# Transposing the softmax weights on TensorE instead of by DMA in the odd head pairs of the first batch

## The chip, the cores and the metric

The kernel runs on one core of a Trainium2 chip. The metric is the device time of one execution in microseconds. It is given as the median of runs; a profile comes from one further execution.

## What is computed

The reference is attention with RMS-normalised queries and keys, followed by a two-layer network with ELU. There are 8 batches, 12 heads, 448 positions and a head size of 64; the network goes from 768 to 2048 and back to 768.

```python
q_n, k_n = rmsnorm(q, g_q), rmsnorm(k, g_k)
scores = matmul(q_n, k_n.T) / sqrt(64)
attn = exp(scores - max(scores))
attn = attn / (sum(attn) + 1e-9)
x = matmul(attn, v)                # then heads side by side: 3584 x 768
h = x @ w_in
g = where(h > 0, h, exp(min(h, 0)) - 1)
out = g @ w_out
```

## The kernel before, in words

All products are made from float16 numbers in two parts, a high one and a low one that holds what the high one lost. Three products (high by high, high by low, low by high) stand for one in float32.

**Attention.** Heads are taken in pairs, 6 pairs to a batch, 48 in all. A pair has 896 query rows, cut into 7 chunks of 128. A chunk T passes through these steps, each on its engine: `s_mm` (TensorE, the scores into a PSUM bank), `s_max` (VectorE, L547), `s_exp` (ScalarE, L553, in place, with the row sum), `s_z` (GpSimd, L557, the sum scaled), `s_rec` (VectorE, L564, 1/z), `s_hi` (ScalarE, L571, the high part of the weights times 1/z), `s_lo` (VectorE, L576, the low part) and `s_tr` (SP, L586, a DMA transpose of both parts into `pts`, the keys on partitions). A pair's transposes go into two buffers, one a head, which the next pair takes over once `attend` has read them. `attend(p)` (TensorE, L597) multiplies the transposed weights by v into the bank `av`, in 22 products of 64 output rows; `x_high` (ScalarE, L604) and `x_low` (VectorE, L608) then read `av`.

**Weights.** The network's weights are converted in the kernel, `w_in` in 16 tiles (`conv_in`) and `w_out` in 24 (`conv_out`). Each is loaded, decoded (`s_act`, ScalarE, L230 and L231), put together (`s_join` and `s_sign`, VectorE, L236 and L260), and summed by column on TensorE (`s_sums`, L135) into columns 448 to 511 of a bank; `s_scale` takes the largest sum (VectorE, L138) and makes a scale from it. From the eighth tile of `w_out` on this bank is `av`, whose columns 0 to 447 belong to `attend`.

**The network.** Its products for one batch (`mlp`, L682 and L696) are spread over the attention of the next batch, from half step 92 on. ScalarE and VectorE make g from each bank (L621 to L637).

**Order.** The program is a list of half steps h, two to a chunk and 14 to a pair. In every half step each engine's work is written in a fixed order: loads; the steps of the chunks (the maximum in even half steps, the exponential in odd ones, `s_hi` two chunks behind in the even ones, `s_lo` in the odd ones); other tasks by a table of half steps (`at`, `steps_at`); then on TensorE the network's products, `s_mm` and `attend`; then TensorE's own tasks (`s_sums` and others). Engines take their lists in order, and SP, which issues all DMAs, does too. `attend(p)` is in half step 7 of the next pair, `x_high` in 8, `x_low` in 9. `s_sums` of every fourth tile of `w_out` is in half step 6 and its `s_scale` in 8. Score banks: 5 in the first batch, 4 afterwards. In the first batch the untransposed weights lie in 8 buffers in `gall`, later in a ring of 3 (`p16`).

The stretches of the profile below are called by pairs: pair 0 begins with the first maximum at 23 us, pair 1 at 46, pair 3 at 90, pair 5 at 133, pair 6 (the second batch) at 157, pair 7 at 185, pair 8 at 216, pair 9 at 245 and pair 10 at 273. A chunk's later steps fall into the stretch after its maximum, and so does `attend`.

Of the kernel before, what the change touches and what calls it, by code (L numbers as in the profile page):

```python
# [32 lines left out]
def tile_attention_then_elu_mlp(ctx: ExitStack, tc: tile.TileContext, qk, v, v_scan, gg, w_in, w_out, out):  # L33
# [12 lines left out]

    nc = tc.nc
# [16 lines left out]
    def t_s(T):  # L64
        return sb[T % (5 if T < PB else 4)]
# [42 lines left out]
    pfirst = cols(gall, NF)[8:]  # L108
# [102 lines left out]
    def conv(src, i, width, acol, bank, parts):  # L211
# [47 lines left out]
        def s_sign():  # L259
# [6 lines left out]
            (-(10, 6, 7)[min(max(i - 2, 0), 2)] if width == WI_W else 0 if i == 1 else -1, load), (3, s_act), (4, s_join), (5, s_sign), (6, on_pe(s_sums)),  # L266
            (7 if width == WI_W else 8, s_scale),
# [6 lines left out]
    def conv_in(f):  # L274
        hi, lo = (t[f].rearrange("p c n -> p (c n)") for t in (whi, wli))
        half = [slice(0, 384), slice(384, 768)]
        dgw = None
        pss = [None, None]

        def s_diag(w, ws):  # L280
            nonlocal dgw
# [16 lines left out]

        return conv(

            w_in, f, WI_W, a_in[:, f : f + 1], sb[4 - f] if f < 2 else av,
            [(9, s_diag), (9, s_high), (11, on_pe(s_low)), (12, lambda w, ws: s_out(0)),
             (13, lambda w, ws: s_out(1))],
        )

    def conv_out(i):
# [22 lines left out]
        def s_store(w, ws):  # L329
# [4 lines left out]
            [(9, s_mult), (10, s_high), (11, s_low), (12, s_store)],  # L334
# [6 lines left out]
    vscale, mscale, vpow = {}, {}, {}  # L341

# [151 lines left out]
    def m_scale(b):  # L494

        p2 = vpow[b]
        if b == 0:
            ibits(a_in, a_in, POWER, ALU.bitwise_and, 0, ALU.bitwise_or)  # L500
        am = small("am")
        nc.vector.tensor_reduce(out=am, in_=a_in, axis=AX.X, op=ALU.max)
        sc, isc = small("sc", NF), small("isc", NF)
        gsc = small("gsc", NF)
        nc.vector.tensor_scalar(
            out=sc, in0=a_in, scalar1=p2, scalar2=2.0 ** (-28 - UP), op0=ALU.mult, op1=ALU.mult
        )
        ibits(isc, sc, -1, ALU.mult, 254 * E, ALU.add)
        nisc = small("nisc", NF)
        nc.vector.tensor_scalar(out=nisc, in0=isc, scalar1=-1.0, scalar2=None, op0=ALU.mult)  # L510

        u = small("u", bufs=3)
        nc.vector.tensor_scalar(
            out=u, in0=am, scalar1=p2, scalar2=2.0 ** (-12 - UP), op0=ALU.mult, op1=ALU.mult
        )
        ui = small("ui")
        ibits(ui, u, -1, ALU.mult, 254 * E, ALU.add)
        nc.vector.tensor_scalar(out=gsc, in0=sc, scalar1=ui, scalar2=None, op0=ALU.mult)
        mscale[b] = [sc, isc, nisc, gsc, u]
# [30 lines left out]

    def s_exp(T):
        ps, st = pss[T][:, :S], stats[T]
        nc.scalar.activation(ps, ps, AF.Exp, bias=st[:, 0:1], accum_out=st[:, 1:2])  # L553

    def s_z(T):
        st = stats[T]
        nc.gpsimd.tensor_scalar(  # L557
            out=st[:, 1:2], in0=st[:, 1:2], scalar1=1e-9, scalar2=2.0**-7, op0=ALU.add, op1=ALU.mult
# [186 lines left out]
    for b in range(B):  # L745
# [5 lines left out]
        at(HB * (b + 1), m_scale, b)  # L751
# [24 lines left out]
    for h in range(H0, LAST):  # L776
# [3 lines left out]
        if odd:  # L780
# [31 lines left out]
        for k in range(parts):  # L812
# [58 lines left out]
```

## Time and profile before

| | us |
|---|---|
| median of 3 runs | 1283.19 (1283.15 to 1283.57) |
| the profiled execution | 1282.81 |
| span of its profile | 1280.8 |
| TensorE busy | 1190.4 (93%) |
| ScalarE busy | 877.9 (69%) |
| VectorE busy | 857.5 (67%) |
| GpSimd busy | 534.7 (42%) |

The span runs from the first to the last instruction of the profiled execution. Busy time is the time in which an engine has an instruction in work; for TensorE the ends of products are modelled. In the rows PE is TensorE (PEld its loading of weights), DVE is VectorE, ACT is ScalarE, POOL is GpSimd, and SP issues DMAs; L and a number is a line of the kernel; `out<-in` names what an instruction writes and reads. PEclk is the clock granted to TensorE as a share of 2.4 GHz. A wait names the instruction that ended it.

### The profile page before, as it was taken

Reading aid. Unit: us, or ns where it says so; the run is one execution under the profiler, and the core shown is the slowest. Engines: PE = TensorE matmul, PEld = TensorE weight load, DVE = VectorE, ACT = ScalarE, POOL = GpSimd, SP = SyncE. Lnnn points to the kernel's source line nnn. Section 1 sums busy time; section 2 is a strip of 40 time slices with the busy share of each in tenths; the row PEclk is TensorE's granted clock in tenths of the full one; section 3 lists DMA queues with packets and bytes.
Section 4 is the critical chain, followed back from the end, with each engine's and each line's share of the span. In section 5 each row is a group of like instructions: output and inputs, shape, how many; then the busy total and the mean of one; then the engine's idle time right before and its main releaser. Section 6 shows DMA issues by size and latency. Waiting matters only on the chain.

```text
span 1280.8 us, 21526 instructions
## 1 busy us (share of the span) xinstructions
PE 1190.4 (93%) x6976; PEld 718.8 (56%) x6976; DVE 857.5 (67%) x1913; ACT 877.9 (69%) x1889; POOL 534.7 (42%) x843
## 2 busy tenths in 40 slices
PE   3667478899999999999999999999999999999998
PEld 2334144466555765577556755576557755676576
DVE  7878988986777567756686567756775768642310
ACT  6898869984788558865796578855886579643520
POOL 3676866674444343343434443434334344320000
PEclk9878679999999999999999999999999999999999
DMA  8999988889877997889788986799678977663011
GB/s 276 223 234 245 231 185 191 201 210 244 161 142 149 229 190 138 153 188 211 151 157 164 221 166 146 146 211 203 135 161 172 213 160 159 140 148 80 1 48 62
DMA packets 452559, 219.22 MB, mean 171 GB/s; under 512 B 408672, under 2 KB 428768, under 8 KB 452448
## 3 DMA queue, kind: packets, MB, share of 16 engines
q1 hardware_dynamic: 452448, 217.86, 78.1%
q8 instruction: 55, 0.90, 0.3%
q14 instruction: 56, 0.46, 0.1%
HBM read 93.52 MB, written 14.16 MB: 84 GB/s over the span
## 4 chain that ended last, share of the span: by engine, by line
PE 76%; DVE 14%; ACT 5%; DMA 3%; issue 2%; SPq 0%; POOL 0%; ACTq 0%; DVEq 0%
PE m L696 21%; PE m L682 20%; PE s L682 10%; PE s L696 9%; PE s L540 8%; PE av L597 7%; DVE w32s L260 2%; DMA pt<-p 2%; DVE wts L236 2%; DVE st L547 2%; DVE p L576 1%; ACT w32s L231 1%; DVE gall L576 1%; ACT wts L230 1%; DVE gall L637 1%
## 5 line engine op out<-in xcount | busy, mean ns | idle before, releaser
L547 DVE TENSOR_REDUCE st<-s 128x1 f32<-128x448 f32 x336 | 208.4, 620 | 174.0 <-PE s L540 173.0
L557 POOL TENSOR_SCALAR st<-st 128x1 f32<-128x1 f32 x336 | 87.4, 260 | 554.8 <-ACT s L553 551.4
L682 PE MATMUL m<-x,whi 128*128 128x448 f16 x1020 | 280.9, 352 | 1.4 <-DVE e L629 1.4
L696 PE MATMUL m<-gall,whos 128*128 128x448 f16 x1024 | 281.7, 353 | 0.0
L571 ACT ACTIVATE p<-s,st 128x448 f16<-128x448 f32 x294 | 186.0, 633 | 112.9 <-DMA pt<-p 89.5
L696 PEld LDWEIGHTS <-whos 128*128 128x128 f16 x1536 | 221.6, 145 | 72.4
L553 ACT ACTIVATE s<-s,st 128x448 f32<-128x448 f32 x336 | 203.2, 605 | 64.5 <-DVE st L547 58.9
L682 PEld LDWEIGHTS <-whi 128*128 128x128 f16 x1536 | 150.2, 98 | 140.7 <-issue 4.5
L576 DVE SCALAR_TENSOR_TENSOR p<-s,st,p 128x448 f16<-128x448 f32 x294 | 196.5, 668 | 31.2 <-ACT p L571 30.0
L540 PE MATMUL s<-qkt 128*128 128x448 f16 (+1 forms) x768 | 188.1, 366 | 16.4 <-DVE gall L576 10.3
L696 PE MATMUL m<-gall,wls 128*128 128x448 f16 x512 | 181.3, 354 | 0.0
L682 PE MATMUL m<-x,wli 128*128 128x448 f16 x510 | 179.9, 353 | 0.0
L682 PE MATMUL s<-x,whi 128*128 128x448 f16 x516 | 141.8, 352 | 0.9 <-DVE e L629 0.9
L696 PE MATMUL s<-gall,whos 128*128 128x448 f16 x512 | 141.2, 353 | 0.4 <-DVE gall L637 0.4
L696 PEld LDWEIGHTS <-wls 128*128 128x128 f16 x768 | 110.5, 144 | 42.7 <-issue 8.2
L597 PE MATMUL av<-pt,vt 128*64 128x448 f16 x1056 | 114.6, 364 | 3.9 <-DVE a_in L138 2.0
L682 PEld LDWEIGHTS <-wli 128*128 128x128 f16 x768 | 75.1, 98 | 74.6 <-issue 7.5
L637 DVE SCALAR_TENSOR_TENSOR gall<-e,gsc,gall 128x448 f16<-128x448 f32 x128 | 97.3, 760 | 29.1 <-ACT gall L634 29.0
L540 PEld LDWEIGHTS <-qkt 128*128 128x128 f16 (+1 forms) x768 | 63.4, 102 | 84.8 <-issue 39.4
L634 ACT ACTIVATE gall<-e,gsc 128x448 f16<-128x448 f32 x128 | 85.1, 665 | 17.8 <-DVE e L629 17.7
L604 ACT ACTIVATE x<-av 128x448 f16<-128x448 f32 x48 | 26.1, 545 | 103.6 <-PE av L597 103.6
L625 ACT ACTIVATE e<-e,nisc,isc 128x448 f32<-128x448 f32 x128 | 96.9, 757 | 0.3
(110 smaller groups left out, 1715.3 us busy)
## 6 DMA issues: line engine op xcount, KB each, us to landing
wls<-wl_d SPq DMA_DIRECT2D x48, 512.0 KB, 4.0
nat<-in_qk SPq DMA_DIRECT2D x48, 448.0 KB, 3.7
raws<-in_w_out SPq DMA_DIRECT2D x24, 512.0 KB, 4.3
qkt<-qkt SPq DMA_DIRECT2D x96, 112.0 KB, 2.3
out<-y SPq DMA_DIRECT2D x48, 224.0 KB, 2.5
vn<-in_v SPq DMA_DIRECT2D x38, 256.0 KB, 3.6
vscan<-in_v_scan SPq DMA_DIRECT2D x36, 224.0 KB, 3.8
whos<-in_w_in SPq DMA_DIRECT2D x10, 768.0 KB, 5.1
```

Of the source, the lines that this page charges most:

```text
L540: nc.tensor.matmul(ps[r0 : r0 + n, :S], lhs, qq[:, 1, h * S : h * S + S], start=(t == 0), stop=(t == 2),)
L547: nc.vector.tensor_reduce(out=st[:, 0:1], in_=pss[T][:, :S], axis=AX.X, op=ALU.max, negate=True)
L553: nc.scalar.activation(ps, ps, AF.Exp, bias=st[:, 0:1], accum_out=st[:, 1:2])
L557: nc.gpsimd.tensor_scalar(out=st[:, 1:2], in0=st[:, 1:2], scalar1=1e-9, scalar2=2.0**-7, op0=ALU.add, op1=ALU.mult)
L571: nc.scalar.activation(p16[:, :S], pss[T][:, :S], AF.Copy, scale=stats[T][:, 2:3])
L576: nc.vector.scalar_tensor_tensor(out=p16[:, S:], in0=ps[:, :S], scalar=r, in1=p16[:, :S], op0=ALU.mult, op1=ALU.subtract)
L597: nc.tensor.matmul(av[64 * h : 64 * h + 64, :S], vt[p][:, j + NJ * i, h], pt[h][:, j, :], start=(k == 0), stop=(k == len(terms) - 1),)
L625: nc.scalar.activation(e, e, AF.Identity, scale=isc, bias=nisc)
L634: nc.scalar.activation(g[:, 0], e, AF.Copy, scale=gsc)
L637: nc.vector.scalar_tensor_tensor(out=g[:, 1], in0=e, scalar=gsc, in1=g[:, 0], op0=ALU.mult, op1=ALU.subtract)
L682: nc.tensor.matmul(ph[:, :S], w[:, c, :], x[:, r, :], start=(c == 0 and i == 0), stop=last)
L696: nc.tensor.matmul(py[:, :S], w, g[:, r, :], start=(f == 0 and i == 0), stop=last)
```

## The change

In the first batch's odd pairs (1, 3 and 5) the DMA transposes go. `s_exp` writes its result to SBUF (`ex`), GpSimd puts 1/z on the diagonal of a 128 x 128 matrix (`s_diag`), and TensorE multiplies (`s_pe`): four chunks of 112 keys are the stationary operands and the diagonal the moving one, in float32, so that the weights come out turned and scaled, in the chunk's own bank, 112 x 4 x 128. `s_hi` and `s_lo` read this bank, one chunk later than before, into `pt_pe` (the upper half of `gall`), and `attend` takes 24 products of 112 keys from there. v is laid out for it by the host, and `v_shift`'s two copies on GpSimd fall away for these pairs. The even pairs of the first batch keep the DMA; their buffers are now 5, one in `gall` and four in `xs`.

Three things go with it. Five score banks are used up to chunk 46 instead of 41. `s_scale` of every fourth tile of `w_out` is in half step 7 of a pair, not 8. The eight small VectorE instructions that make a batch's scales (`m_scale`, now `m_steps`) are spread over eight half steps, one to each, 16 half steps ahead of the batch's end on, instead of all at the end.

```diff
     def t_s(T):
-        return sb[T % (5 if T < PB else 4)]
+        return sb[T % (5 if T < PB + 5 else 4)]
...
-    pfirst = cols(gall, NF)[8:]
+    pt_pe = gall[:CK, 8 * 2 * S :].rearrange("p (i c q) -> p i c q", i=2, c=4)
+
+    pfirst = [gall[:, NPAIR * 1024 : NPAIR * 1024 + 2 * S]]
+    pfirst += [t.rearrange("p i s -> p (i s)") for t in xs[NPAIR - 1 :]]
...
-            (7 if width == WI_W else 8, s_scale),
+            ... (scale, s_scale),
...
             w_out, i, WO_W, most[:, i : i + 1], mb[i % 2] if i < WO_OWN else av,
-            [(9, s_mult), (10, s_high), (11, s_low), (12, s_store)],
+            [(9, s_mult), (10, s_high), (11, s_low), (12, s_store)], scale=7 if i % 4 == 3 else 8,
...
     def v_shift(p):
+        if by_pe(p * NJ):
+            return
...
+    def by_pe(T):
+        return T < PB and T // NJ % 2 == 1
+
     def s_exp(T):
         ps, st = pss[T][:, :S], stats[T]
-        nc.scalar.activation(ps, ps, AF.Exp, bias=st[:, 0:1], accum_out=st[:, 1:2])
+        e = ps
+        if by_pe(T):
+            e = es[T] = pool.tile([128, 2 * S], F16, tag="p16", name="ex", bufs=3).bitcast(F32)
+        nc.scalar.activation(e, ps, AF.Exp, bias=st[:, 0:1], accum_out=st[:, 1:2])
...
+    def s_diag(T):
+        dg = dgs[T] = pool.tile([128, 128], F32, tag="dgz", name="dgz", bufs=2)
+        nc.gpsimd.tensor_scalar(
+            out=dg, in0=ident, scalar1=stats[T][:, 2:3], scalar2=0.0, op0=ALU.mult, op1=ALU.add
+        )
+
+    def s_pe(T):
+        e, dg = es.pop(T), dgs.pop(T)
+        for c in range(4):
+            nc.tensor.matmul(
+                pss[T][:CK, c * 128 : c * 128 + 128], e[:, c * CK : c * CK + CK], dg,
+                start=True, stop=True,
+            )
...
     def s_hi(T):
+        if by_pe(T):
+            ps, hi, _ = turned(T)
+            nc.scalar.activation(hi, ps, AF.Copy)
+            return
...
     def s_lo(T):
+        if by_pe(T):
+            ps, hi, lo = turned(T)
+            del pss[T], stats[T]
+            nc.vector.tensor_tensor(out=lo, in0=ps, in1=hi, op=ALU.subtract)
+            return
...
-            if ok(T - 2):
-                s_lo(T - 2)
-
-                if T % NJ == 1:
-                    s_tr(T - 2)
+            for t in (T - 3, T - 2):
+                if ok(t) and by_pe(t) == (t == T - 3):
+                    s_lo(t)
...
+            if ok(T - 2) and by_pe(T - 2):
+                s_diag(T - 2)
...
+        if odd and ok(T - 2) and by_pe(T - 2):
+            s_pe(T - 2)
         run_tasks(h, 2)
...
+CK = S // 4
```

How instructions move, at three places.

TensorE, pair 1, around the `attend` that reads the weights of pair 0: L597 is `attend` and L540 `s_mm`. Before:

```order
L597 MATMUL av<-pt,vt 64x448
L540 LDWEIGHTS qkt
L540 MATMUL s_69<-qkt 128x448
L540 LDWEIGHTS qkt
L540 MATMUL s_69<-qkt 128x448
L540 LDWEIGHTS qkt
L540 MATMUL s_70<-qkt 128x448
```

And after the change, with L660 for `attend`, L557 for `s_mm` and L601 for `s_pe`:

```order
L660 MATMUL av<-pt,vt 64x448
L601 MATMUL s_70<-dgz,ex 112x128 x4
L557 LDWEIGHTS qkt
L557 MATMUL s_69<-qkt 128x448
L557 LDWEIGHTS qkt
L557 MATMUL s_69<-qkt 128x448
L601 MATMUL s_71<-dgz,ex 112x128 x4
```

The transpose of one chunk stands directly behind `attend`, ahead of the next scores, and that of the next chunk behind these.

VectorE, pair 7, around the maximum of the twelfth tile of `w_out` (`most<-av`, with the `ws` and `a_out` that follow from it). Before:

```order
L564 RECIPROCAL st<-st 128x1
L576 SCALAR_TENSOR_TENSOR p_2025<-s_69,st,p_2025 128x448
L629 SCALAR_TENSOR_TENSOR e<-e,m_74 128x448
L547 TENSOR_REDUCE st<-s_68 128x1
L138 TENSOR_REDUCE most<-av 128x1
L144 TENSOR_SCALAR ws<-most 128x1
L144 TENSOR_SCALAR a_out<-most 32x3 x4
L236 SCALAR_TENSOR_TENSOR wts<-wts,w32s 128x512
```

And after:

```order
L590 RECIPROCAL st<-st 128x1
L630 SCALAR_TENSOR_TENSOR p_2142<-s_69,st,p_2142 128x448
L143 TENSOR_REDUCE most<-av 128x1
L149 TENSOR_SCALAR ws<-most 128x1
L149 TENSOR_SCALAR a_out<-most 32x3 x4
L692 SCALAR_TENSOR_TENSOR e<-e,m_74 128x448
L564 TENSOR_REDUCE st<-s_68 128x1
L241 SCALAR_TENSOR_TENSOR wts<-wts,w32s 128x512
```

The maximum moves from behind the score maximum of the next half step to directly behind `s_lo`, one half step earlier. At the five such places `attend` now follows it in the program.

TensorE, pair 7: the last product of `s_mm` and the beginning of `attend`, with what each instruction waits for. Before:

```order
L540 LDWEIGHTS qkt
L540 MATMUL s_68<-qkt 64x448
L597 LDWEIGHTS vt [waits DMAHW7_49,DMAHW2_49,Pool_49]
L597 MATMUL av<-pt,vt 64x448 [waits DMAHW0_49]
L597 LDWEIGHTS vt [waits DMAHW4_49,DMAHW1_49]
L597 MATMUL av<-pt,vt 64x448 [waits DMAHW0_49]
```

And after:

```order
L557 LDWEIGHTS qkt
L557 MATMUL s_68<-qkt 64x448
L660 LDWEIGHTS vt [waits DMAHW2_49,DMAHW7_49,DMAHW0_49,Pool_49]
L660 MATMUL av<-pt,vt 64x448 [waits DVE_49]
L660 LDWEIGHTS vt [waits DMAHW4_49,DMAHW1_49]
L660 MATMUL av<-pt,vt 64x448 [waits DMAHW0_49]
```

The first product waits for VectorE, where it waited only for DMA queues.

## Rows read from the trace of the kernel before

**Rows 1.** The page, part 2: busy tenths in 40 slices of the span.

```profile
PE   3667478899999999999999999999999999999998
```

**Rows 2.** Busy time by stretch, one pair each; columns in the first line.

```profile
core 0: us, PE busy (x) PEld busy (x) DVE busy (x) ACT busy (x) POOL busy (x), PEclk, DMA share, GB/s
46.26:68.45 22.19, 14.69 (x95) 7.95 (x95) 17.84 (x40) 18.70 (x42) 18.86 (x23) 0.88 0.95 227
90.39:113.00 22.61, 15.23 (x96) 8.41 (x96) 18.60 (x43) 19.27 (x44) 15.98 (x20) 0.80 1.08 255
133.17:157.12 23.95, 11.18 (x75) 5.15 (x74) 21.63 (x45) 18.85 (x41) 19.45 (x25) 0.64 1.09 250
157.12:185.40 28.28, 19.40 (x123) 9.72 (x123) 22.90 (x54) 18.11 (x41) 18.05 (x23) 0.70 0.87 207
185.40:215.71 30.31, 26.65 (x171) 13.57 (x170) 26.47 (x60) 27.19 (x57) 20.08 (x25) 0.94 0.83 167
215.71:245.03 29.32, 24.86 (x171) 12.81 (x169) 26.31 (x56) 26.93 (x57) 18.12 (x23) 1.00 0.92 224
272.89:296.02 23.13, 22.95 (x148) 16.13 (x146) 18.29 (x44) 16.39 (x37) 17.61 (x25) 1.00 0.92 214
```

**Rows 3.** Waits of VectorE, 23 to 165 us: total, times, longest.

```profile
DVE wts L236 <- ACT w32s L231: 15.3, 13, 1.8
DVE mv L173 <- DMA whos<-in_v: 1.5, 1, 1.5
```

**Rows 4.** Waits of VectorE, 165 to 300 us.

```profile
DVE most L138 <- ACT x L604: 14.0, 5, 3.8
```

**Rows 5.** Timeline, pair 7: start, duration, engine, line, operation, tiles, idle before.

```profile
198.52 3.60 PE L597 MATMUL av<-pt,vt 128*64 128x448 f16 x22
198.74 0.67 DVE L576 SCALAR_TENSOR_TENSOR p<-s,st,p 128x448 f16<-128x448 f32 x1
202.77 0.23 DVE L138 TENSOR_REDUCE most<-av 128x1 f32<-128x64 f32 x1 [2.30 <-ACT x L604]
205.46 0.61 DVE L608 TENSOR_TENSOR x<-av,x 128x448 f16<-128x448 f32 x1
```

**Rows 6.** Timeline, pair 8.

```profile
228.34 2.25 PE L597 MATMUL av<-pt,vt 128*64 128x448 f16 x22
229.86 0.66 DVE L576 SCALAR_TENSOR_TENSOR p<-s,st,p 128x448 f16<-128x448 f32 x1
233.82 0.23 DVE L138 TENSOR_REDUCE most<-av 128x1 f32<-128x64 f32 x1 [2.77 <-ACT x L604]
```

**Rows 7.** Timeline, pair 6: ScalarE's wait for a transpose.

```profile
178.94 0.64 ACT L571 ACTIVATE p<-s,st 128x448 f16<-128x448 f32 x1 [3.48 <-DMA pt<-p]
```

**Rows 8.** Timeline, pair 6: two of the scales, and GpSimd.

```profile
159.96 1.03 POOL L419 TENSOR_TENSOR t<-nat,t 128x448 f16<-128x448 f32 x1
160.01 1.01 DVE L144 TENSOR_SCALAR isc<-sc 128x16 int32<-128x16 int32 x1
161.06 0.17 DVE L510 TENSOR_SCALAR nisc<-isc 128x16 f32<-128x16 f32 x1
```

**Rows 9.** Timeline, pair 3: the first product after attend, and ScalarE.

```profile
101.96 0.93 PE L540 MATMUL s<-qkt 128*128 128x448 f16 x4
102.15 0.65 ACT L571 ACTIVATE gall<-s,st 128x448 f16<-128x448 f32 x1
```

**Rows 10.** Timeline of TensorE, pair 3: float32 passes.

```profile
97.41 0.81 PE L293 MATMUL m<-w32s,dgw 128*128 128x384 f32 x2
98.06 0.33 PE L294 MATMUL m<-whi,neg 128*128 128x384 f16 x1
```

**Rows 11.** Groups by line and form, 23 to 165 us: ScalarE, GpSimd.

```profile
L571 ACT ACTIVATE gall<-s,st 128x448 f16<-128x448 f32 x42 | 26.8, 638 | 8.3 <-issue 4.2 <-ACT s L553 3.0 <-DVE st L564 0.9
L604 ACT ACTIVATE x<-av 128x448 f16<-128x448 f32 x5 | 2.8, 550 | 0.2 <-PE av L597 0.2
L464 POOL COPY vt<-vt 64x384 f16<-64x384 f16 x12 | 7.8, 652 | 0.6
```

More of the change, by code (lines that the diff above doesn't have):

```diff
@@ L209, in tile_attention_then_elu_mlp, with conv @@
     most = const.tile([128, 4 * NC_], F32, name="most")
-    def conv(src, i, width, acol, bank, parts):
+    def conv(src, i, width, acol, bank, parts, scale=8):
         raw = raw_in[i % len(raw_in)] if width == WI_W else room(raws, 2 * width, i)
@@ L303, in conv_in @@
              (13, lambda w, ws: s_out(1))],
+            scale=7,
         )
@@ L492, in v_steps, with m_steps, mul, powers @@
         return [(0, one), (1, two), (4, on_pe(three)), (5, four)]
[L494 to L519, printed above, removed]
+    def m_steps(b):
+        sc, isc, nisc, gsc, u, am, ui = m = [
+            small(n, NF if n.endswith("c") else 1, bufs=3 if n == "u" else 2)
+            for n in ("sc", "isc", "nisc", "gsc", "u", "am", "ui")
+        ]
+        mscale[b] = m[:5]
+        def mul(out, x, s1, s2=None):
+            nc.vector.tensor_scalar(
+                out=out, in0=x, scalar1=s1, scalar2=s2, op0=ALU.mult,
+                **({} if s2 is None else {"op1": ALU.mult}),
+            )
+        def powers():
+            if b == 0:
+                ibits(a_in, a_in, POWER, ALU.bitwise_and, 0, ALU.bitwise_or)
+        def most_of():
+            nc.vector.tensor_reduce(out=am, in_=a_in, axis=AX.X, op=ALU.max)
+        return list(enumerate([
+            powers, most_of,
+            lambda: mul(sc, a_in, vpow[b], 2.0 ** (-28 - UP)),
+            lambda: ibits(isc, sc, -1, ALU.mult, 254 * E, ALU.add),
+            lambda: mul(nisc, isc, -1.0),
+            lambda: mul(u, am, vpow[b], 2.0 ** (-12 - UP)),
+            lambda: ibits(ui, u, -1, ALU.mult, 254 * E, ALU.add),
+            lambda: mul(gsc, sc, ui),
+        ]))
     def cuts(j):
@@ L557, in s_z @@
         nc.gpsimd.tensor_scalar(
[L558 removed]
+            out=st[:, 1:2], in0=st[:, 1:2], scalar1=1e-9,
+            scalar2=2.0 ** (UP - 7) if by_pe(T) else 2.0**-7, op0=ALU.add, op1=ALU.mult,
         )
@@ L590, in attend @@
     def attend(p):
-        pt = [pts.pop(2 * p), pts.pop(2 * p + 1)]
-        terms = [(j, i) for j in range(4) for i in (0, 1)] + [(j, 0) for j in range(4, NJ)]
-        for k, (j, i) in enumerate(terms):
+        if by_pe(p * NJ):
+            pt = [[pt_pe[:, i, :, h * S : h * S + S] for h in (0, 1)] for i in (0, 1)]
+            terms = [
+                (vt[p][:CK, j + NJ * i], [t[:, j] for t in pt[k]])
+                for j in range(4) for i, k in ((0, 0), (1, 0), (0, 1))
+            ]
+        else:
+            pt = [pts.pop(2 * p), pts.pop(2 * p + 1)]
+            terms = [(j, j + NJ * i) for j in range(4) for i in (0, 1)]
+            terms += [(j, j) for j in range(4, NJ)]
+            terms = [(vt[p][:, i], [t[:, j] for t in pt]) for j, i in terms]
+        for k, (vs, ps) in enumerate(terms):
             for h in (0, 1):
                 nc.tensor.matmul(
-                    av[64 * h : 64 * h + 64, :S], vt[p][:, j + NJ * i, h],
-                    pt[h][:, j, :], start=(k == 0), stop=(k == len(terms) - 1),
+                    av[64 * h : 64 * h + 64, :S], vs[:, h], ps[h], start=(k == 0),
+                    stop=(k == len(terms) - 1),
                 )
@@ L765, in tile_attention_then_elu_mlp @@
         steps_at(WO_START + 14 * (i // 4) + (0, 3, 7, 10)[i % 4], conv_out(i))
+    for b in range(B):
+        at(HB * (b + 1) - 17, lambda b=b: steps_at(HB * (b + 1) - 16, m_steps(b)))
     def mlps():
@@ L784, in tile_attention_then_elu_mlp @@
                 s_rec(T - 1)
-            if ok(T - 2):
-                s_lo(T - 2)
-                if T % NJ == 1:
-                    s_tr(T - 2)
+            for t in (T - 3, T - 2):
+                if ok(t) and by_pe(t) == (t == T - 3):
+                    s_lo(t)
+            if ok(T - 2) and T % NJ == 1 and not by_pe(T - 2):
+                s_tr(T - 2)
         else:
@@ L794, in tile_attention_then_elu_mlp @@
                 s_z(T - 1)
-            if ok(T - 2):
-                s_hi(T - 2)
+            if ok(T - 2) and by_pe(T - 2):
+                s_diag(T - 2)
+            for t in (T - 3, T - 2):
+                if ok(t) and by_pe(t) == (t == T - 3):
+                    s_hi(t)
             for t in (T - 4, T - 3):
-                if ok(t) and t % NJ != NJ - 1 and (t % NJ == 0) == (t == T - 4):
+                if ok(t) and t % NJ != NJ - 1 and (t % NJ == 0) == (t == T - 4) and not by_pe(t):
                     s_tr(t)
```

15 lines of the change are left out of this document (11 added, 4 removed).

## The prediction

> **What bounds the kernel now.** I read the profile in the order page, busy time by stretch, waits, timeline.
>
> On the page the reader sees TensorE at 9 tenths or more from the eleventh slice on [rows 1]: from about 296 us the kernel is bound by TensorE, whose work there is the same in both kernels. A change can gain only by letting that full stretch begin earlier. So everything is decided in the first 296 us, by pairs 0 to 10.
>
> The busy time by pair of heads [rows 2] says who limits each of them. In pairs 1 and 3 (22.2 and 22.6 us) VectorE and ScalarE are each busy for 17.8 to 19.3 us, and TensorE for 15. In pairs 7 and 8 (30.3 and 29.3 us) ScalarE works 27.2 and 26.9 us and VectorE 26.5 and 26.3: both are nearly full, and each pair takes 6 to 7 us more than the 23.13 of pair 10, where TensorE is full. So two engines that wait for each other set the pace, not one; freeing one of them is worth only what the other has idle.
>
> The waits say what they wait for. In pairs 0 to 5 VectorE waits 15.3 us for ScalarE's decoding of the weights, and only 1.5 us for a DMA [rows 3]. From 165 to 300 us two thirds of its idle time is one wait: the column maximum `most<-av` waits 14.0 us in 5 places [rows 4] for `x_high`, that is for `attend`, which shares the bank.
>
> **The change part by part.** The sum is made against the profiled execution (1282.81 us; its span 1280.8); the median of the runs lies 0.4 us above it.
>
> *The maximum ahead of attend: -5.0 us.* With `scale=7` the maximum of every fourth converted tile stands before `attend` in the order, and needs just the column sums, which TensorE has done before it begins `attend`. All 14.0 us go. But `attend` now waits for that read (the order shows a wait on VectorE that was not there). In pair 7 TensorE began `attend` at 198.52 and took 3.5 us; VectorE's place for the maximum is now behind the subtraction that ends at 199.41 [rows 5], so `attend` begins at about 199.7 and ends at 203.2, 1.1 us later than now. `x_high` on ScalarE (0.55 [rows 11]) ends at 203.8 and `x_low` starts then, not at 205.46: VectorE gains 1.6 us, ScalarE loses 1.1. In pair 8 `attend` moves from 228.34 to about 230.8 and takes 2.2 us: it ends at 233.0, before ScalarE comes to `x_high` (it ended at 233.8, when the maximum could start) [rows 6]. There VectorE gains all its 2.8 us and ScalarE loses nothing. In pair 10 TensorE is full, so its wait of a microsecond buys nothing. Ends: a gain of 10.5 us, if each place gives what VectorE waited and ScalarE had idle (3.8, the longest [rows 4], 2.3 and 2.4 in pairs 7 and 8, some 2 in a fourth); a loss of 4, if TensorE's later start of 1 us a place is handed on. I take 1.25 us for each of pairs 6 to 9, between the two places worked out.
>
> *Chunk 42's transposes: -1.5 us.* They write the buffers that `attend` of pair 5 reads, so they are issued after it, and ScalarE waits 3.48 us for their landing before it can reuse the space they read [rows 7]. Pair 5 no longer uses these buffers. ScalarE is not the fuller engine in pair 6 (18.1 of 28.3 us), so I take less than half. Ends: 0 and -3.5.
>
> *The scales in eight steps: -0.5 us.* Eight VectorE instructions that stood in a row in pair 6 move into pair 5, one to a half step. VectorE is the fullest engine in both pairs [rows 2], so their time is paid either way. One took 1.01 us where the next, on the same 16 columns, took 0.17 [rows 8]; it can shrink, or two others swell as much. Ends: -0.8 and +1.7.
>
> *Five banks up to chunk 46: +1.0 us.* After it chunks 48 and 49 take banks used three chunks earlier, so their products stand in the same half step as the subtraction that frees the bank. A product takes 0.93 us [rows 9]. VectorE waits for between 0 and 0.93 of it, twice, with the hops; I take 0.5 each. Ends: 0 and +2.
>
> *The transpose on TensorE: +3.0 us.* The nearest rows are the float32 products of the weights' low halves: two passes of 384 columns from 97.41 to 98.06, 0.325 us each [rows 10], at 2.4 GHz. For 128 columns that is 0.108, and 8 passes a chunk make 0.87 us, 1.73 at 1.2 GHz. If each pass also shows its weight load of 128 columns (another 0.1), 1.7 and 3.5. Seven chunks a pair are 6 us at the low end, inside the 7.4 us that TensorE has idle in pair 3 [rows 2]. On the path lies one place a pair: the step stands behind `attend` of the even pair, and ScalarE's `s_hi` behind it. In pair 3 `attend` ends at 101.96 and ScalarE came to its `s_hi` at 102.15 [rows 9]; now it waits until 102.9 to 103.8. I take 1.0 us for each of three odd pairs. Ends: 0 (ScalarE waits for VectorE a little later anyway) and +10 (3.5 us a chunk, less 0.2, three times).
>
> *What the DMA queues no longer carry: -1.0 us.* 24 of the 48 transposes of pairs 0 to 5 go, and SP no longer stands at them ahead of the loads. DMA is at a share of 0.95 to 1.09 there [rows 2], yet VectorE's one wait for it is 1.5 us [rows 3]. Ends: 0 and -5.
>
> *Small ones: -0.3 us.* `s_hi` without a scale costs what `x_high` does: 550 ns for 448 columns, some 600 for 512, against 638 [rows 11]; 21 times, -0.8 us on ScalarE. `s_lo` on 512 columns is `x_low` (0.61 us for 448 [rows 5]) and a seventh: 0.69 for 0.67, +0.5 us on VectorE. The 21 diagonals on GpSimd take about 0.3 us each, by their 128 columns against its 1.03 us for 448 [rows 8]; 6 copies of 0.65 go [rows 11]. GpSimd's two more microseconds hide in its idle time (6.6 of 22.6 us in pair 3).
>
> A row speaks against that last point: the 1.01 us instruction ended as GpSimd's multiplication from 159.96 to 160.99 ended [rows 8]. The Trainium skill (SBUF — State Buffer, SBUF: two separate sides) says that VectorE and GpSimd share a pair of ports, held for a whole instruction. By it each diagonal could hold VectorE for its own length, at most 21 x 0.3 us, against 6 x 0.65 no longer held: +2.4 instead of nothing.
>
> Sum: -5.0 - 1.5 - 0.5 + 1.0 + 3.0 - 1.0 - 0.3 = -4.3 us, so 1278.5 for the profiled execution and **1278.9** for the median.
>
> **The rivals.**
> - *The barrier was all (more gain).* VectorE's 14.0 us come off wherever ScalarE has room, 10.5 us in all: 1278.9 - 5.5 = 1273.4. For it: the wait joins three engines at one point. Against: ScalarE is at 27 of 30 us in pair 7.
> - *The wait only moves (no change).* TensorE's wait for the maximum and ScalarE's for `x_high` take the first term to 0: 1283.9. For it: pair 7 as worked out.
> - *TensorE binds the odd pairs (slower).* The point is 1.06 us a chunk: above it seven chunks exceed the 7.4 us idle in pair 3. At 1.2 GHz the 0.87 becomes 1.73, 12.1 us a pair: 4.7 too many in pair 3, 4.6 in pair 1 (7.5 idle), none in pair 5 (12.8 idle). That is 9.3 where I had 2.0: 1286.2. For it: the clock granted in these pairs is 0.64 to 0.88. Against: a busier TensorE was granted more (1.00 in pair 10). The Trainium skill (TensorE: Matmul & The Clock Gate, Part 1) says that activity releases the throttle; by it the added work would itself lift the clock, as the rows of pairs 5 and 10 agree.
>
> **How the numbers follow.** A measurement of this kernel tells 0.2%, 2.6 us, from no change: faster is below 1280.6, slower above 1285.8. Forecast 0.45 (its own range 1275 to 1282, with 0.40 below 1280.6), more gain 0.15, moved wait 0.20 (0.16 within), TensorE bound 0.20 (0.16 above, the rest within). Faster 0.55; same 0.05 + 0.16 + 0.04 = 0.25; slower 0.04 + 0.16 = 0.20. The range runs from 1270, past the larger gain, to 1288, past TensorE bound.
>
> **What would show it.** Right: no `most<-av` wait for `x_high`, and a new wait of `attend` on VectorE of 1 to 2.5 us in pairs 6 to 10; these pairs 1 to 2 us shorter; the odd pairs up to 1 us longer, with ScalarE waiting for TensorE once in each; eight passes of 0.1 us a chunk. Wrong: ScalarE's `s_hi` waiting for TensorE in most chunks, or pairs 7 to 9 still at 28 to 30 us, or under 27; or odd pairs shorter than now, which would mean that the DMA bound them.

## The result, and the profile after

The change took 1288.12 us (median, 1285.67 to 1289.71) beside 1283.57 for the kernel before (1282.65 to 1286.16): a ratio of 1.0031, 95% interval 1.0019 to 1.0042. By the ratio it is slower by 0.3%, 4.0 us (the two medians lie 4.6 apart), where 4.3 us of gain were forecast. The profiled execution took 1287.62 us (its span 1285.8).

TensorE's slices on the page of the change:

```profile
PE   3668679899999999999999999999999999999998
```

In both kernels the stretch of nines begins in the ninth slice, at about 256 us [rows 1], not in the eleventh, where the prediction read it. From the first score maximum of pair 12 to the end the kernel before took 960.2 us and the change 959.8, so all of the difference lies before it, as the prediction had it. Busy time by pair in the change (columns as in [rows 2]; pairs 1, 3, 5, 6, 7, 8 and 10):

```profile
46.27:72.33 26.06, 20.17 (x122) 13.49 (x123) 17.77 (x40) 18.40 (x41) 20.09 (x26) 0.81 0.71 196
...
95.93:119.32 23.39, 19.30 (x134) 12.85 (x135) 18.75 (x42) 18.70 (x43) 16.77 (x23) 0.86 0.78 213
...
142.18:166.50 24.32, 15.33 (x96) 9.46 (x96) 20.79 (x51) 16.95 (x38) 21.15 (x27) 0.64 0.64 168
166.50:193.94 27.44, 22.15 (x139) 13.04 (x140) 20.30 (x47) 19.81 (x43) 20.03 (x28) 0.77 0.78 194
193.94:222.63 28.69, 27.28 (x193) 15.17 (x192) 28.38 (x58) 26.35 (x55) 18.91 (x24) 1.00 0.75 187
222.63:251.39 28.76, 24.31 (x159) 13.34 (x157) 27.30 (x57) 26.14 (x54) 17.14 (x22) 0.94 0.80 200
...
279.96:302.77 22.81, 22.21 (x144) 16.17 (x143) 20.17 (x45) 16.52 (x37) 18.00 (x25) 1.00 0.87 203
```

Pair 1 grew from 22.2 to 26.1 us [rows 2], though no engine is full in it: TensorE works 20.2, GpSimd 20.1, ScalarE 18.4 and VectorE 17.8. The DMA's share fell from 0.95 to 0.71 and nothing became shorter for it. Pairs 6 to 8 shrank by 0.8, 1.6 and 0.6. Over pairs 1 to 5 the change takes 120.23 us, where the kernel before took 110.86; over pairs 6 to 11, 159.49 where it took 163.54. So in these two profiles 9.4 are lost and 4.0 won; how far such sums scatter is told with the experiments. (A pair is timed here from the first `st<-s` maximum of its seven on VectorE to that of the next.)

What the waits say of the first stretch, 23 to 175 us of the change (us in total, times, longest):

```profile
PE s L601 <- POOL dgz L594: 16.4, 9, 3.2
...
ACT gall L614 <- PE s L601: 14.0, 10, 2.4
...
DVE wts L241 <- ACT w32s L236: 16.5, 15, 1.8
DVE a_in L143 <- PE av L140: 5.6, 2, 4.6
...
POOL st L582 <- ACT ex L578: 9.1, 9, 2.4
```

A chain is to be read here: TensorE waits for GpSimd's diagonal (`dgz`), ScalarE's `s_hi` waits for TensorE, and VectorE waits for TensorE's column sums. VectorE's old wait for the decoding (15.3 [rows 3]) is still there, and the one for the column sums was 0.4 us before; the first two are new. These waits are not a sum of losses: from 23 to 175 us TensorE stood idle for 45.6 us in all, and for 57.1 in the kernel before. The last line is GpSimd's own: `s_z` of the next chunk (`st`), which stands directly ahead of the diagonal, waits for that chunk's exponential. One place, pair 1, in the timeline:

```profile
50.22 1.05 POOL L474 COPY vt<-vt 64x384 f16<-64x384 f16 x2
...
51.37 1.48 POOL L291 TENSOR_SCALAR whi<-w32s,ws 128x768 f16<-128x768 f32 x1
...
52.93 0.20 POOL L582 TENSOR_SCALAR st<-st 128x1 f32<-128x1 f32 x1
...
53.23 0.38 POOL L594 TENSOR_SCALAR dgz<-ident,st 128x128 f32<-128x128 f32 x1
...
53.66 2.05 PE L601 MATMUL s<-dgz,ex 128*112 128x128 f32 x8 [3.23 <-POOL dgz L594]
...
55.50 1.49 PE L298 MATMUL m<-w32s,dgw 128*128 128x384 f32 x2
...
55.74 0.60 ACT L614 ACTIVATE gall<-s 112x512 f16<-112x512 f32 x1 [2.37 <-PE s L601]
```

The diagonal itself takes 0.38 us, and the reciprocal that it needs had been there since 49.45. But it stands behind two copies of `v`, the high half of a weight tile (`whi`) and the next chunk's `z`, 3.0 us of a queue (50.22 to 53.23). TensorE was idle for 3.23 us before the passes, and then made the eight passes at a granted clock of 0.50, which is 1.2 GHz: 2.05 us. ScalarE waited 2.37 us for the chunk.

The second stretch, 165 to 326 us of the change:

```profile
PE av L660 <- DVE most L143: 7.7, 5, 2.2
...
ACT p L620 <- DMA pt<-p: 11.6, 6, 4.2
ACT x L667 <- PE av L660: 7.6, 5, 2.6
```

VectorE's wait for `x_high` (14.0 us [rows 4]) is gone. In its place stand a new wait of `attend` for VectorE (7.7) and a longer one of `x_high` for `attend` (7.6, where it was 3.4).

### The profile page after: what moved, and what is told of

It is laid out like the page before. It is cut to its first block, busy times and chain, and to the rows that moved or that the text cites. A ratio compares the mean times of both kernels' runs of the same rounds, so it can differ in the third digit from the quotient of the medians.

```text
span 1285.8 us, 21847 instructions
## 1 busy us (share of the span) xinstructions
PE 1207.0 (94%) x7150; PEld 743.0 (58%) x7150; DVE 852.3 (66%) x1913; ACT 880.1 (68%) x1889; POOL 538.2 (42%) x858
## 4 chain that ended last, share of the span: by engine, by line
PE 80%; DVE 11%; ACT 3%; issue 2%; POOL 2%; DMA 1%; SPq 0%; ACTq 0%; POOLq 0%; DVEq 0%
PE m L759 22%; PE m L745 20%; PE s L759 11%; PE s L745 11%; PE s L557 8%; PE av L660 7%; DVE w32s L265 2%; DVE st L564 1%; DVE wts L241 1%; DVE p L630 1%; PE s L601 1%; ACT w32s L236 1%; DVE gall L700 1%; DVE ss L379 1%; ACT wts L235 1%
## 5 line engine op out<-in xcount | busy, mean ns | idle before, releaser
L582 POOL TENSOR_SCALAR st<-st 128x1 f32<-128x1 f32 x336 | 83.3, 248 | 560.2 <-ACT s L578 542.3
L578 ACT ACTIVATE s<-s,st 128x448 f32<-128x448 f32 x315 | 190.3, 604 | 65.3 <-DVE st L564 63.1
L557 PE MATMUL s<-qkt 128*128 128x448 f16 (+1 forms) x768 | 186.6, 362 | 9.7 <-DVE gall L627 4.9
L700 DVE SCALAR_TENSOR_TENSOR gall<-e,gsc,gall 128x448 f16<-128x448 f32 x128 | 95.3, 745 | 26.1 <-ACT gall L697 26.1
L660 PE MATMUL av<-pt,vt 128*64 128x448 f16 x990 | 105.0, 359 | 5.8 <-DVE most L143 5.8
L557 PEld LDWEIGHTS <-qkt 128*128 128x128 f16 (+1 forms) x768 | 63.4, 101 | 73.1 <-issue 29.2
L667 ACT ACTIVATE x<-av 128x448 f16<-128x448 f32 x48 | 26.1, 544 | 110.9 <-PE av L660 110.9
L697 ACT ACTIVATE gall<-e,gsc 128x448 f16<-128x448 f32 x128 | 85.0, 664 | 20.4 <-DVE e L692 20.1
```

What stands on the lines that cost most here:

```text
L557: nc.tensor.matmul(ps[r0 : r0 + n, :S], lhs, qq[:, 1, h * S : h * S + S], start=(t == 0), stop=(t == 2),)
L578: nc.scalar.activation(e, ps, AF.Exp, bias=st[:, 0:1], accum_out=st[:, 1:2])
L582: nc.gpsimd.tensor_scalar(out=st[:, 1:2], in0=st[:, 1:2], scalar1=1e-9, scalar2=2.0 ** (UP - 7) if by_pe(T) else 2.0**-7, op0=ALU.add, op1 ...
L660: nc.tensor.matmul(av[64 * h : 64 * h + 64, :S], vs[:, h], ps[h], start=(k == 0), stop=(k == len(terms) - 1),)
L697: nc.scalar.activation(g[:, 0], e, AF.Copy, scale=gsc)
L700: nc.vector.scalar_tensor_tensor(out=g[:, 1], in0=e, scalar=gsc, in1=g[:, 0], op0=ALU.mult, op1=ALU.subtract)
```

## The experiments

Labels stand for the kernels. The ratios are to the kernel before, timed on the same chip in the same session. Not all kernels ran in one session, so ratios are compared, not times. The last columns are sums of the pairs' times in one profile each. Those sums scatter: pairs 1 to 3, which `before_scale7`, `rest_only`, `rest_scale8`, `spread_only` and `banks_only` leave as they were, took 66.9 to 69.5 us in these and 66.7 in the kernel before (`before_scale7` was expected to keep them within 0.5 us and had 68.7). So a difference under 3 us in the sums says nothing, and up to 3 of the 9.4 us lost in pairs 1 to 5 may be scatter: the one profile of the kernel before has the shortest pairs 1 to 3 of the six.

| label | ratio, 95% interval | pairs 1-5, us | pairs 6-11, us |
|---|---|---|---|
| before | 1 | 110.9 | 163.5 |
| the change | 1.0031 [1.0019, 1.0042] | 120.2 | 159.5 |
| const_diag | 0.9977 [0.9968, 0.9987] | 112.7 | 159.7 |
| diag_vec | 1.0003 [0.9992, 1.0013] | 116.5 | 157.6 |
| diag_early | 0.9982 [0.9972, 0.9993] | 113.4 | 158.7 |
| pe_last | 1.0035 [1.0023, 1.0047] | 120.5 | 161.0 |
| scale8 | 1.0018 [1.0005, 1.0031] | 120.0 | 159.3 |
| before_scale7 | 0.9996 [0.9985, 1.0007] | 111.9 | 164.4 |
| rest_only | 0.9991 [0.9980, 1.0002] | 112.8 | 161.0 |
| rest_scale8 | 0.9975 [0.9966, 0.9984] | 110.9 | 159.7 |
| scales_at_once | 1.0055 [1.0039, 1.0071] | 117.9 | 163.1 |
| spread_only | 0.9979 [0.9971, 0.9988] | 115.3 | 160.2 |
| banks_only | 0.9987 [0.9977, 0.9996] | 112.2 | 162.0 |
| early_scale8 | 0.9960 [0.9948, 0.9972] | 113.9 | 156.9 |
| one_pair | 0.9984 [0.9973, 0.9995] | 112.2 | 161.6 |
| one_pair_scale8 | 0.9968 [0.9957, 0.9979] | 112.6 | 157.3 |

**Is it the diagonal?** `const_diag` gives TensorE one constant diagonal in place of the 21 that GpSimd makes, so 1/z is left out in those chunks:

```
...
     def s_pe(T):
-        e, dg = es.pop(T), dgs.pop(T)
+        e, dg = es.pop(T), dgc
...
-            if ok(T - 2) and by_pe(T - 2):
-                s_diag(T - 2)
```

> Left out: 1/z; the diagonal is a constant 4 made once, so the weights are turned but not normalised, and GpSimd's 21 diagonals and TensorE's wait for them go, while the 168 float32 passes, the later s_hi and s_lo and everything else stay. Theory A (the first batch lost 9.4 us because TensorE, which takes its list in order, waits for GpSimd's diagonal, 16.4 us in 9 places, and the scores, column sums and attend behind it come late): TensorE's waits before L601 fall under 3 us, pairs 1 to 5 come back to 21 to 23 us each, and the kernel is 6 to 9 us faster than the change, 1279 to 1282. Rival B (the passes themselves, 1.0 us a chunk at 2.4 GHz and 2.0 at 1.2, fill TensorE in the odd pairs): at most 2 us faster than the change, 1286 to 1288. Rival C (the ring of steps became one chunk longer and the five banks are too few): also under 3 us faster, with waits of the scores L557 for VectorE's subtraction in place of those for the diagonal.

It took 1281.3 us, a ratio of 0.9977. All 168 passes remain, and yet pairs 1 to 5 go from 120.2 to 112.7. So neither TensorE's added work nor the form of the transposes makes the loss; what makes it is that the diagonal is made, or where.

`diag_vec` makes it on VectorE, right behind the reciprocal:

```
-        nc.gpsimd.tensor_scalar(
+        nc.vector.tensor_scalar(
...
                 s_rec(T - 1)
+                if by_pe(T - 1):
+                    s_diag(T - 1)
...
```

> The diagonal is made by VectorE directly behind the reciprocal instead of by GpSimd one half step later. Theory A: TensorE's waits before L601 fall from 16.4 to under 4 us; VectorE pays 21 instructions of 0.1 to 0.25 us, 2 to 5 us, part of it on the path; 3 to 7 us faster than the change, 1281 to 1285. Rivals B and C: no gain, and VectorE's added work shows: 1288 to 1292.

1285.1 us, a ratio of 1.0003. The diagonal is on time (TensorE waits for it once, 1.1 us), but VectorE, the fullest engine, pays 10.0 us for the 21 instead of 2 to 5: 0.29 us for eleven of them, 0.39 to 1.06 for the rest. Pairs 1 to 5 take 116.5.

**The place in GpSimd's queue, or its load?** `diag_early` leaves the diagonal on GpSimd and moves it half a step ahead, to the same place in the order as `diag_vec`, and so ahead of the copies and the weight tile:

```
                 s_rec(T - 1)
+                if by_pe(T - 1):
+                    s_diag(T - 1)
...
-            if ok(T - 2) and by_pe(T - 2):
-                s_diag(T - 2)
```

> The change, but GpSimd makes each diagonal half a step earlier, right behind the reciprocal it needs, ahead of the copies of v, the join and the next chunk's sums. Theory A: TensorE's wait for the diagonal falls from 16.4 to under 5 us, pairs 1 to 5 from 120.2 to 112.5 to 115 us (the constant diagonal had 112.7), 1281 to 1284. Theory B (GpSimd has no place for 21 more instructions, wherever they stand: each now waits there for the reciprocal and holds the next sums up instead): the wait only changes its name, GpSimd's wait for VectorE's reciprocal takes 5 us or more, pairs 1 to 5 stay at 118 or above, 1286 to 1288.

1280.7 us, a ratio of 0.9982. The same work on the same engine at another place takes back 6.3 us (1.0031 less 0.9982, of 1283), give or take 2 by the two intervals. Its waits, 23 to 175 us:

```profile
PE s L557 <- DVE gall L627: 14.2, 11, 2.9
...
PE s L601 <- POOL dgz L594: 1.7, 3, 1.2
```

The wait for the diagonal falls from 16.4 to 1.7 us, ScalarE's for the passes from 14.0 to 3.9, and GpSimd's `s_z` waits 2.2 us for the exponential, not 9.1. TensorE now waits 14.2 (1.5 in the change) for banks that VectorE has not freed: it is ahead of the others. The same place of pair 1:

```profile
50.66 0.37 POOL L594 TENSOR_SCALAR dgz<-ident,st 128x128 f32<-128x128 f32 x1
...
51.08 1.13 PE L601 MATMUL s<-dgz,ex 128*112 128x128 f32 x8
51.09 1.86 POOL L474 COPY vt<-vt 64x384 f16<-64x384 f16 x2
```

Counted from the pair's first maximum (46.27 in the change, 46.79 here) the diagonal is there 3.1 us sooner, the passes run at a granted clock of 1.00 (2.4 GHz), and the chunk costs 1.13 us, not 2.05. Theory B of that expectation, that GpSimd has no room, falls: with no diagonals on GpSimd at all (`const_diag`, 0.9977) the kernel is not measurably faster than with the early ones.

**Who suffers from TensorE's wait?** `pe_last` puts the passes behind TensorE's other tasks of the half step:

```
+        run_tasks(h, 2)
         if odd and ok(T - 2) and by_pe(T - 2):
             s_pe(T - 2)
-        run_tasks(h, 2)
```

> The change, but in each half step of an odd pair TensorE's transposes of the weights (s_pe) stand behind the column sums and the converted tiles' low products instead of ahead of them. Theory A (TensorE, taking its instructions in order, stands at s_pe for GpSimd's diagonal, 16.4 us, and holds up what is behind it): VectorE's wait of 5.6 us for the column sums goes, but ScalarE's wait for s_pe, 14.0 us, stays or grows by up to a microsecond a place, since the diagonal comes no earlier. If the column sums were what hurt: pairs 1 to 5 at 114 to 117 us together instead of 120.2, and 1283 to 1285. If ScalarE's wait was what hurt: 119 to 122 and 1287 to 1289. Theory C (not the diagonal's lateness but TensorE's added 6 us a pair): no difference, 1288.

1287.5 us, as the change. VectorE's wait for the column sums fell from 5.6 to 1.5 us, and ScalarE's rose:

```profile
ACT gall L614 <- PE s L601: 16.0, 10, 3.9
```

So what was queued behind the passes seems to cost nothing, and the late chunk itself does. That is argued: one wait fell as the other rose, and an exchange that cancels out would look the same. Theory C there fits this time too; `const_diag` and `diag_early` rule it out.

**The maximum ahead of attend.** `scale8` is the change with `scale=8` for all tiles; `before_scale7` is the kernel before with `scale=7` for every fourth.

```
-            [(9, s_mult), (10, s_high), (11, s_low), (12, s_store)], scale=7 if i % 4 == 3 else 8,
+            [(9, s_mult), (10, s_high), (11, s_low), (12, s_store)], scale=8,
```

> The change with the maximum of every fourth tile of w_out back in half step 8, behind attend: that part alone undone. If the part is worth the 5.0 us of the prediction, the 14 us of VectorE's waits for x_high come back, attend no longer waits for VectorE (7.7 us in 5 places), and the kernel is 4 to 6 us slower than the change, 1292 to 1294. If the wait only moved, within 1.5 us of the change, 1287 to 1289.

> The kernel before with that one part of the change alone: the maximum of every fourth tile of w_out in half step 7. If the part is worth what the prediction took (5.0 us): 1277 to 1280. If the wait only moved: 1282.5 to 1284.5. In either case the first batch up to attend of pair 4 keeps its times within 0.5 us.

1286.4 and 1283.8 us. In `scale8` VectorE's old wait is back (11.2 us in 5 places) and that of `attend` is gone, and yet the kernel is not slower. Alone the move is worth nothing (0.9985 to 1.0007), and the change looks better off without it, though these two intervals overlap. The same step was then taken beside the other parts: `early_scale8` is `diag_early` with `scale=8`.

> The change with the diagonal half a step earlier (1280.7 us) and scale=8 again for every tile, so that the column maximum stands behind attend. Without the early diagonal scale=8 took 1.7 us off the change, to the kernel before scale=7 added nothing. Theory F (a read ahead of attend costs TensorE what it gives VectorE, or more): 1278.5 to 1281. Theory of the prediction (5.0 us gained by it, here covered by the diagonal's wait until that went): 1283 to 1286.

1279.1 us, the fastest ratio of all, 0.9960. Each of the four pairs of kernels that differ in `scale=7` beside the spread scales reads the same way: the change and `scale8` (1.0031, 1.0018), `diag_early` and `early_scale8` (0.9982, 0.9960), `rest_only` and `rest_scale8` (0.9991, 0.9975), and, with one more small difference, the two with one pair (0.9984, 0.9968). `scale=7` costs 0.13 to 0.22%, 1.7 to 2.8 us. No one pair has intervals that are clearly apart, and the two of a pair ran in different sessions; four of four on one side is what the statement rests on. How the waits trade places is seen in `rest_scale8`, 165 to 326 us:

```profile
DVE most L138 <- ACT x L611: 12.1, 5, 2.8
...
DVE st L554 <- PE s L547: 2.7, 3, 1.1
...
ACT x L611 <- PE av L604: 2.9, 2, 1.7
```

and in `rest_only`, the same with `scale=7`:

```profile
PE av L604 <- DVE most L138: 7.5, 4, 2.3
...
ACT x L611 <- PE av L604: 8.7, 6, 2.3
...
DVE st L554 <- PE s L547: 5.6, 7, 1.0
```

VectorE sheds 12.1 us of one wait. TensorE takes on 7.5, ScalarE 5.8, and VectorE itself waits 5.6 for scores, where it waited 2.7.

**The gain in pairs 6 to 11.** `rest_only` is the kernel before with all of the change but the transposes, `scales_at_once` the change with the eight instructions in a row again:

```
-        at(HB * (b + 1) - 17, lambda b=b: steps_at(HB * (b + 1) - 16, m_steps(b)))
+        for _, step in m_steps(b):
+            at(HB * (b + 1), step)
```

> The kernel before, with everything of the change except the transposes on TensorE: scale=7 for every fourth tile, the scales in eight steps, five banks up to chunk 46; all 48 transposes of pairs 0 to 5 stay with the DMA. Pair 6 took 28.3 us before, 27.4 in the change and 25.7 with the constant diagonal. Theory D (the 4 us that the change gains in pairs 6 to 11 are from chunk 42's transposes, which no longer wait for pair 5's attend): pair 6 stays at 28 to 29 us, 1283 to 1284, and ScalarE's wait of 3.5 us for pt is still there. Theory E (they are from the banks and the spread scales): pair 6 at 25.5 to 27, pairs 1 to 5 at 110 to 112 together, 1279.5 to 1281.5. My own steps of the prediction gave banks +1.0 and scales -0.5, so 1284.

> The change, with the eight instructions of the scales in a row at the batch's end again, as before the change. By the prediction's step (-0.5 us): 1288.5 to 1289. Theory E: pair 6 rises by 1 to 2 us from 27.4, 1289 to 1290. Theory D: pair 6 within 0.6 us of 27.4, 1288.

1281.6 and 1289.7 us. Pair 6 takes 26.2 us with all but the transposes, and 28.2 with the scales in a row. So its gain does not come from chunk 42's transposes. The two parts alone, `spread_only` (four banks, `scale=8`) and `banks_only` (`T < PB + 5` and nothing else):

> The kernel before with one part of the change alone: the eight instructions of the scales one to a half step. Pair 6 took 28.3 us in the kernel before and 26.2 with all of the change but the transposes. Theory E1 (the spreading made that gain): pair 6 at 26 to 26.7 us, pairs 6 to 11 at 161 to 162 together instead of 163.5, 1281 to 1282. Theory E2 (the fifth bank made it): pair 6 at 28 to 29, 1282.5 to 1283.5. The prediction's step (-0.5): 1282.

> The kernel before with another part alone: five banks up to chunk 46 instead of 41. Theory E1: pair 6 stays at 28 to 29 us, 1282.5 to 1283.5. Theory E2: pair 6 at 26 to 26.7, 1281 to 1282. The prediction's step (+1.0): pairs 6 and 7 a microsecond longer together, 1283.5 to 1284.

1281.1 and 1282.9 us, and pair 6 at 25.8 and 28.4: the spreading does it. In all sixteen profiles pair 6 takes 25.3 to 27.4 us with the scales spread, and 28.2 to 28.7 in the four without. Why is read in the kernel before, pair 6. On VectorE the eight stand between a score maximum and a chunk's `s_lo`, and TensorE waits for the bank which that `s_lo` frees. VectorE's timeline:

```profile
158.65 0.99 DVE L144 TENSOR_SCALAR a_in<-a_in 128x16 int32<-128x16 int32 x1
...
161.57 0.23 DVE L518 TENSOR_SCALAR gsc<-sc,ui 128x16 f32<-128x16 f32 x1
161.72 0.16 DVE L564 RECIPROCAL st<-st 128x1 f32<-128x1 f32 x1
161.79 0.67 DVE L576 SCALAR_TENSOR_TENSOR gall<-s,st,gall 128x448 f16<-128x448 f32 x1
```

TensorE, at the same place:

```profile
162.51 0.90 PE L540 MATMUL s<-qkt 128*128 128x448 f16 x2 [6.23 <-DVE gall L576]
```

From 158.65 to 161.72 VectorE does nothing for the scores; those 3.1 us are half of the 6.23 for which TensorE stood idle. In `spread_only`, with the eight gone from there, the same place shows the other half:

```profile
163.93 0.90 PE L547 MATMUL s<-qkt 128*128 128x448 f16 x2 [3.14 <-DVE gall L583]
```

**Are the transposes worth anything once the diagonal is early?** `rest_scale8` is `early_scale8` without them. `one_pair` keeps them in pair 5 alone (`return T // NJ == 5`), with the early diagonal and `scale=7`; in it pairs 1 and 3 pair the weights with rows of `v` that lie in the other layout, the work being the same. The untransposed weights of pairs 0 to 4 all go through the change's 5 buffers there, where the kernel before had 8. `one_pair_scale8` has `scale=8` and the rows of `v` in their place.

> The change with the diagonal half a step earlier, but TensorE transposes in pair 5 alone; pairs 1 and 3 go back to the DMA, 10 chunks fewer on TensorE (14). Pairs 1 to 4 took 90.1 us with the early diagonal, 86.9 in the kernel before, 89.5 with all of the change but the transposes. Theory G (what is left of the loss is in the transposes themselves): pairs 1 to 4 at 87 to 89, 1278 to 1280. Theory H (it is in the other parts, or none is left): pairs 1 to 4 at 89.5 to 90.5, 1280 to 1282. Theory I (the DMA, relieved, gave something in those pairs): over 90.5, 1281 to 1283.

> The kernel before with the spread scales and the fifth bank alone: scale=8, all transposes of pairs 0 to 5 with the DMA. It is early_scale8 (ratio to the kernel before 0.9960) without the transposes on TensorE. Theory J (the transposes are worth nothing, the two small parts are all): the product of the two parts' own ratios, 0.9979 x 0.9987 = 0.9966, so 1279 to 1280.5, pairs 6 to 11 at 157 to 159. Theory K (the transposes free the DMA and chunk 42's wait, and are worth 1.5 to 4 us with the diagonal early): 0.998 to 0.999, 1281 to 1283. Theory F has rest_only (0.9991, scale=7) slower than this by about 2 us.

> The change with the diagonal half a step earlier and scale=8, TensorE's transposes in pair 5 alone, and pairs 1 and 3's rows of v laid out for the DMA's transposes. Theory J: as rest_scale8 within 0.1%. Theory K by way of chunk 42's wait: as early_scale8 or better, 0.9945 to 0.9965, 1277 to 1279.5; by way of the DMA's relief in all odd pairs: between the two.

The ratios are 0.9984, 0.9975 and 0.9968. `one_pair` beside `diag_early` (0.9982) shows no difference, which was theory H; its pairs 1 to 4 took 88.8 us, as theory G had it, but a difference of 1.3 us in such a sum says nothing. For `scale=8`: with the transposes 0.9960, without 0.9975, with a third of them 0.9968: in order, by 1.9 us from end to end, but the intervals overlap (0.9948 to 0.9972 against 0.9966 to 0.9984). Theory J, nothing at all, gave 0.9966 from the product of the parts, and this measured a little worse; theory K gave 0.998 to 0.999, and this measured better. What the transposes are worth, between nothing and some 4 us, stays open. Against the change, `early_scale8` is 0.7% faster (1.0031 less 0.9960).

## Why the prediction was wrong

**What bounds the kernel** was right: the result was decided before pair 12, and two or three engines that wait for each other set the pace there.

**The step that failed** is the sentence that "GpSimd's two more microseconds hide in its idle time", in the term "small ones: -0.3 us". On it rests the term "the transpose on TensorE: +3.0 us", whose path has one place a pair and no wait for the diagonal. Idle time of an engine (6.6 of 22.6 us in pair 3 [rows 2]) says that work fits, not that it is done in time. I costed GpSimd's 21 diagonals by their length and their room, and did not ask what stands ahead of them in its queue, what that in turn waits for, and who waits behind. The runs showed in its place: 16.4 us of waits of TensorE, 14.0 of ScalarE, and 6.3 us of the kernel's time, which come back when the order alone is mended.

The price of the passes was right. I had 0.108 us a pass and 0.87 a chunk at 2.4 GHz, 1.73 at 1.2; the passes follow each other every 0.109 us at 2.4 GHz and 0.213 at 1.2, and a chunk, with the end of its last pass, takes 1.04 to 1.13 and 1.92 to 2.05. I had ScalarE wait in one place a pair, behind `attend`; it waited for the passes in ten places, and TensorE for the diagonal in nine.

**The maximum ahead of attend, -5.0 us:** right that the wait would go and that `attend` would wait for VectorE instead, 1 to 2.5 us a place (7.7 us in 5 places, 2.2 the longest). Wrong in what remains of it: nothing alone (0.9996), a loss of 1.7 to 2.8 beside the spread scales. I gave VectorE's gain and TensorE's delay from two places, and took ScalarE to be late anyway; its own wait for `attend` rose (from 3.4 to 7.6 us). The rival "the wait only moves" named this, with 0 in place of -5.0.

**The scales in eight steps, -0.5:** -2.7 (0.9979). I wrote that "their time is paid either way" because VectorE is the fullest engine in both pairs. It is the fullest, but in a row they kept TensorE idle for 3.1 of the 6.23 us at one place. That spread out they fall into VectorE's waits is argued, not shown.

**Five banks, +1.0:** -1.7 alone (0.9987), about nothing beside the spread scales (0.9975 with, 0.9979 without). No run shows the cost that I took; whether there is a gain is open, since the first interval (0.9977 to 0.9996) hardly leaves 1 out.

**Chunk 42's transposes, -1.5:** pair 6 took 25.7 us in `rest_scale8`, with all transposes on the DMA, and 25.4 and 25.3 in the two that have pair 5 on TensorE. The 0.3 to 0.4 is within the scatter. ScalarE's 3.48 us [rows 7] was time in which it had nothing to catch up: at the same place it stood idle for 3.50 us in `rest_scale8` (put down to a maximum of VectorE there) and 0.62 in `early_scale8`, and the pair is 0.3 shorter.

**The DMA's relief, -1.0:** not seen. The DMA's share fell in all odd pairs (0.95 to 0.71 in pair 1) and with the diagonal in time pairs 1 to 5 took 113.4 us, against 112.8 with all transposes on the DMA. Together with the transposes themselves it is between nothing and the 4 us of the last experiments.

**The sum by the runs:** all but the transposes 0.9991, the transposes with a timely diagonal 0.9982 / 0.9991, the lateness 1.0031 / 0.9982: -1.2, -1.2 and +6.3 us. That these add up to the measured 4.0 is so by construction, since each ratio begins where the last one ends; and the two small ones are not clear of noise. The forecast had -4.5 for the maximum, the scales and the banks, +0.2 for the transposes and what goes with them, and nothing for lateness. So of the 8.3 us between forecast and measurement 6.3 are the lateness, 3.3 come from the other three parts, and -1.4 from the transposes on time.

**The rival that came nearest in time**, TensorE binding the odd pairs (1286.2), is not what happened. TensorE had 5.9 us idle in pair 1 and 9.0 in pair 5, and with the same passes and a constant diagonal the kernel was faster than before. In its terms, seven chunks a pair did not become 12.1 us: of the 21 chunks 15 were made at or near 2.4 GHz and six at 1.2 GHz or little above. Five of these six had waited for their diagonal, but so had four that were made at 2.4 GHz, one of them after 2.50 us:

```profile
71.09 1.13 PE L601 MATMUL s<-dgz,ex 128*112 128x128 f32 x8 [2.50 <-POOL dgz L594]
```

In `const_diag`, where none waits for a diagonal, two were still made at 0.50. So what sets the rate of a single chunk stays open. The Trainium skill (TensorE: Matmul & The Clock Gate, Part 1) says that activity releases the throttle. In pair 5 of the change that did not show: TensorE worked 15.3 us there, not 11.2, and was granted 0.64 in both; with as much work (15.4 us), but the diagonal in time, `diag_early` was granted 0.72.

## What to carry to other kernels

A small instruction on an engine with idle time is not free when another engine waits for its result: read what stands ahead of it in that queue at the moment its input is ready, and add up those durations and what those instructions wait for, not the engine's idle share. Place it right behind its own input; half a step earlier was worth 6.3 us here, and a row of eight small instructions between a score and the freeing of its bank was worth 2.7 when it was spread out. A wait that joins three engines may go from one and come back on the other two; to price its removal, follow each of the three.

## What the runs showed that I had not expected

Three of the 21 diagonals took 1.15 to 1.39 us, not 0.38. One of them, pair 5 of the change, with VectorE beside it:

```profile
160.43 1.39 POOL L594 TENSOR_SCALAR dgz<-ident,st 128x128 f32<-128x128 f32 x1
...
160.46 0.67 DVE L627 TENSOR_TENSOR gall<-s,gall 112x512 f16<-112x512 f32 x1
161.05 0.61 DVE L418 TENSOR_TENSOR nat<-nat,gst 128x448 f32<-128x448 f32 x1
```

It ends 0.16 us after the second of VectorE's instructions. The other two end 0.15 and 0.16 us after one of VectorE's as well (`wts<-wts,w32s` and `w32s<-raws,wts`). These three of VectorE's read both inputs from SBUF. Beside `gall<-s,gall`, which reads a score bank, diagonals took 0.38 us as ever (at 60.29 and 106.10, for example). Not every overlap costs: at 151.41 a diagonal took 0.38 beside `w32s<-raws,wts`. I had expected VectorE to pay for a conflict; here GpSimd did, by 0.8 to 1.0 us. In `diag_vec`, where VectorE makes the diagonals, VectorE did: ten of the 21 took 0.39 to 1.06 us and ended 0.08 to 0.09 us after an instruction of GpSimd. The Trainium skill (SBUF — State Buffer, SBUF: two separate sides) says that the two share ports, held for a whole instruction. The traces agree that one engine stands until the other's instruction is over; they do not show which of the two has to.
